# Turning the output columns by a VectorE block transpose instead of a masked matmul, in a decode-step attention and FFN kernel

## The chip, the cores and the metric

The kernel runs on one core of one Trainium2 chip. The metric is the device time of one execution in microseconds (us). The time before is 1287.16 us (median of 6 runs, 1286.88 to 1287.58).

## The reference

One token passes an attention layer with a cache of 32768 positions in 32 heads and, in parallel, a gated FFN. The result is one row of 640 values.

```python
xn = layernorm(x)                                  # x: [1, 1, 640], bf16
q = xn @ wq                                        # 32 heads of 128
p = softmax(q . k_cache * 128 ** -0.5)             # k_cache, v_cache: [1, 32, 32768, 128]
attention = (p . v_cache) @ wo                     # wo: [4096, 640]
ffn = (silu(xn @ w_gate) * (xn @ w_up)) @ w_down   # hidden width 1728
return x + attention + ffn                         # [1, 1, 640], bf16
```

The two caches make up nearly all of the 554 MB that are read.

## The kernel before

SyncE issues the loads into a ring of three large slots. VectorE and TensorE form the scores, ScalarE the exponentials, TensorE the weighted sums. The last weights to be loaded are those of `wo`, in six pieces, and the last sums are accumulated in PSUM (the memory that TensorE writes its sums to) as five columns: `acc[m, c]` holds output `c * 128 + m`. The change concerns only how these columns become the output row.

```python
# TensorE: the last projection, then the turning (fold32[p, m] = 1 where p % 32 == m)
project().then_inc(s_att, 1)                       # acc: [128, NCD], NCD = 5
t.wait_ge(s_fin, 1)
t.matmul(orow_ps, lhsT=outb[:, :, :], rhs=fold32[:, :], start=True, stop=True).then_inc(s_or, 1)

# VectorE: blk[p, a] = 1 where p // 32 == a, RB = 4
v.wait_ge(s_att, 1)
v.tensor_tensor(out=outb[:, :, :], in0=acc[:, :, None].to_broadcast([128, NCD, RB]),
                in1=blk[:, None, :].to_broadcast([128, NCD, RB]), op=ALU.mult).then_inc(s_fin, 1)
v.wait_ge(s_or, 1)
v.tensor_copy(out=orow[:, :], in_=orow_ps).then_inc(s_fin, 1)      # orow: [20, 32] bf16

# SyncE: 20 rows on 20 neighbouring partitions
e.wait_ge(s_fin, 2)
e.dma_start(out[0, 0:1, :].rearrange("o (r m) -> (o r) m", m=32), orow[:, :]).then_inc(s_out, 16)

# GpSimd: the program ends when the store has landed
g.wait_ge(s_out, 16)
# ... everything else is cut here ...
```

The mask spreads each column over four columns, one for each group of 32 partitions. The matmul with `fold32` then adds up each of these 20 columns into a row of 32.

## Time and profile before

| What | Value |
|---|---|
| time, median of 6 runs | 1287.16 us |
| span of the profiled execution | 1285.3 us |
| mean DMA rate | 431 GB/s |
| start of the masking to the issue of the store | 0.68 us |
| issue of the store to the end of the span | 1.4 us |

From the page of the kernel before come its busy times by engine, two of its slice lines (each digit is the busy share of a fortieth of the span, in tenths), and its chain of waits (shares of the span).

```profile
span 1285.3 us, 10032 instructions
PE 1041.2 (81%) x5160; PEld 261.3 (20%) x3240; DVE 672.3 (52%) x409; ACT 52.1 (4%) x139; POOL 2.6 (0%) x18
...
DVE  0855665445665446664446664446654446654441
...
DMA  9999999999999999999999999999999999999998
...
DMA 53%; PE 28%; DVE 12%; issue 6%; DVEq 0%; SPq 0%
```

The DMA engines are busy throughout. A change that touches no transfer of the stream can only gain or lose in the stretch after the last load. The timeline of that stretch follows (start, duration, engine, line, operation, result and operands, count; in brackets the idle time before and what ended it).

```profile
1281.73 1.45 PE L451 MATMUL ps<-ot,ring 128*128 128x1 bf16 x40 [0.72 <-DMA ring<-in_A_wo_dram]
1283.22 0.18 DVE L641 TENSOR_TENSOR outb<-ps,blk 128x20 bf16<-128x20 f32 x1 [11.79 <-PE ps L451]
1283.46 0.09 PEld L476 LDWEIGHTS ps<-fold,outb 128*20 128x20 bf16 x1 [0.36 <-DVE outb L641]
1283.46 0.20 PE L476 MATMUL ps<-fold,outb 128*20 128x32 bf16 x1 [0.27 <-DVE outb L641]
1283.70 0.18 DVE L644 CAST orow<-ps 20x32 bf16<-20x32 f32 x1 [0.29 <-PE ps L476]
1283.90 0.39 SPq L255 DMA_DIRECT2D out_dram<-orow  x1
```

After the last projection come three small instructions on two engines, one after the other, and then the store. The view of the DMA engines over 1283.9 to 1285.1 us, also in 40 slices, shows when the store's packets moved.

```profile
DMA  0000000000000000000000000003010000000000
...
DMA packets 30, 0.00 MB, mean 1 GB/s; under 512 B 30, under 2 KB 30, under 8 KB 30
```

The packets lie in the slices from 27 on, about 0.8 us after the issue began. The trace's records tell more: 20 packets of 64 B and 10 of 4 B, the first 0.805 us after the start of the issue, the last 0.081 us later, and GpSimd's wait ends 0.397 us after that. From the start of the issue to this release it is 1.283 us, nearly twice as long as the turning itself (0.679 us). The chain of waits in the page does not show this part, since it begins at the last instruction that computes.

### The profile page before, as it was taken

The numbers are of one execution on the slowest core, as the hardware profiler recorded it, in microseconds if no ns is written. First come the engines' busy times: TensorE is split into PE (matmuls) and PEld (weight loads), VectorE is DVE, ScalarE is ACT, GpSimd is POOL, SyncE is SP. The second block draws the span as 40 slices with busy tenths as digits, with TensorE's granted clock in tenths as the row PEclk, the third lists the DMA queues.
The fourth block names the chain that finished last, engine by engine and source line by source line (L and its number), as shares of the span: only waits on it lengthen the run. The fifth ranks groups of instructions, "written<-read, shape, count | busy, mean of one in ns | idle before, by whom it ended". The sixth has DMA issues, their size and how long they took to land.

```text
span 1285.3 us, 10032 instructions
## 1 busy us (share of the span) xinstructions
PE 1041.2 (81%) x5160; PEld 261.3 (20%) x3240; DVE 672.3 (52%) x409; ACT 52.1 (4%) x139; POOL 2.6 (0%) x18
## 2 busy tenths in 40 slices
PE   3599777789788789778898877798787798778797
PEld 1022112221112221112221112221112221112227
DVE  0855665445665446664446664446654446654441
ACT  2000000000000000000000000000000000000000
POOL 0000000000000000000000000000000000000000
PEclk9799888898888898888998888898888998888995
DMA  9999999999999999999999999999999999999998
GB/s 424 424 447 429 428 437 435 428 432 439 432 432 432 439 428 432 439 432 432 428 443 428 432 439 432 432 426 445 428 432 439 430 434 426 441 432 432 439 419 364
DMA packets 10987, 554.16 MB, mean 431 GB/s; under 512 B 1247, under 2 KB 1504, under 8 KB 1760
## 3 DMA queue, kind: packets, MB, share of 16 engines
q1 hardware_dynamic: 10974, 554.00, 99.7%
q8 instruction: 9, 0.15, 0.0%
q14 instruction: 2, 0.02, 0.0%
q10 hardware_dynamic: 2, 0.00, 0.0%
HBM read 553.99 MB, written 0.00 MB: 431 GB/s over the span
## 4 chain that ended last, share of the span: by engine, by line
DMA 53%; PE 28%; DVE 12%; issue 6%; DVEq 0%; SPq 0%
DMA ring<-in_A_k_cache_dram 51%; PE ps L358 16%; DVE ring L577 12%; PE ps L310 9%; DMA ring<-in_A_wo_dram 2%; PE ps L342 1%; PE ps L329 1%; PE ps L400 0%; PE ps L394 0%; PE ps L388 0%; PE ps L451 0%; SPq L252 0%; DVEq L577 0%; DVE sc L583 0%; DVE pmax L589 0%
## 5 line engine op out<-in xcount | busy, mean ns | idle before, releaser
L577 DVE TENSOR_TENSOR ring<-ring,qb 128x8192 bf16<-128x8192 bf16 x128 | 557.8, 4421 | 315.8 <-DMA ring<-in_A_k_cache_dram 315.8
L310 PE MATMUL ps<-ring,ident 128*128 128x512 bf16 x1920 | 497.2, 418 | 0.0
L358 PE MATMUL ps<-ring,P 128*4 128x512 bf16 x1920 | 429.0, 379 | 0.0
L329 PE MATMUL ps<-ring,ident 128*128 128x512 bf16 x128 | 55.9, 437 | 220.1 <-DVE ring L577 219.8
L358 PEld LDWEIGHTS ps<-ring,P 128*4 128x4 bf16 x1920 | 158.1, 85 | 230.1
L329 PEld LDWEIGHTS ps<-ring,ident 128*128 128x128 bf16 x128 | 12.6, 98 | 617.6 <-issue 309.7
L583 DVE TENSOR_REDUCE sc<-ps 128x64 f32<-128x512 f32 x128 | 82.3, 686 | 62.8 <-PE ps L310 62.8
L595 DVE TENSOR_SCALAR negb<-ps 128x1 f32<-128x1 f32 x32 | 5.1, 159 | 108.4 <-PE ps L400 108.4
L503 ACT ACTIVATE P<-sc,negb 128x256 bf16<-128x256 f32 x32 | 16.2, 508 | 956.9 <-DVE negb L595 956.9
L592 DVE TENSOR_REDUCE m<-ps 1x1 f32<-1x128 f32 x32 | 8.9, 278 | 85.2 <-PE ps L394 85.2
L380 PEld LDWEIGHTS ps<-identf,o 4*128 4x128 f32 x248 | 30.7, 190 | 13.1 <-issue 13.1
L380 PE MATMUL ps<-identf,o 4*128 4x1 f32 x248 | 33.3, 251 | 0.0
L388 PEld LDWEIGHTS ps<-rsum,ones 128*128 128x128 f32 x64 | 12.1, 190 | 99.3 <-issue 98.5
L494 ACT ACTIVATE o<-ps,rzb 4x512 f32<-4x512 f32 x31 | 21.0, 677 | 6.3 <-PE ps L345 6.3
L301 PE MATMUL ps<-ring 128*128 x40 | 10.6, 432 | 11.2 <-DMA ring<-in_A_wq_dram 11.2
L499 ACT ACTIVATE ocol<-ps 128x1 f32 (+1 forms) x31 | 5.4, 173 | 222.4 <-PE ps L380 222.4
L342 PE MATMUL ps<-ring,P 128*4 x64 | 14.4, 379 | 0.0
L589 DVE TENSOR_REDUCE pmax<-sc 128x1 f32<-128x256 f32 x32 | 13.5, 421 | 0.0
L394 PE MATMUL ps<-identf,pmax 128*1 128x128 f32 x64 | 12.2, 272 | 1.2 <-DVE pmax L589 1.2
L400 PE MATMUL ps<-m,ones 1*128 1x1 f32 x64 | 12.1, 256 | 0.4 <-DVE m L592 0.4
L400 PEld LDWEIGHTS ps<-m,ones 1*128 1x128 f32 x64 | 9.4, 183 | 14.0 <-issue 13.3
L565 DVE RECIPROCAL rzb<-ps 128x1 f32<-128x1 f32 x32 | 5.1, 158 | 8.1 <-PE ps L388 8.1
(75 smaller groups left out, 97.3 us busy)
## 6 DMA issues: line engine op xcount, KB each, us to landing
ring<-in_A_v_cache_dram SPq DMA_DIRECT2D x2, 4096.0 KB, 36.5
ring<-in_A_wq_dram SPq DMA_DIRECT2D x1, 5120.0 KB, 15.5
ring<-in_A_wo_dram SPq DMA_DIRECT2D x3, 1280.0 KB, 24.6
ring<-in_B_w_gate_dram SPq DMA_DIRECT2D x1, 2160.0 KB, 22.6
ring<-in_B_w_up_dram SPq DMA_DIRECT2D x1, 2160.0 KB, 27.9
ring<-in_B_w_down_dram SPq DMA_DIRECT2D x1, 2080.0 KB, 31.0
ring<-in_A_wo_dram SPq DMA_DIRECT2D x1, 800.0 KB, 28.7
ring<-in_A_k_cache_dram SPq DMA_DIRECT2D x32, 41.4
```

Source lines behind the costliest of these rows:

```text
L310: return t.add_instruction(mybir.InstMatmult(start_tensor_calc=False, stop_tensor_calc=stop, tile_size=(128, 128), tile_position=(0, 0), l ...
L329: t.matmul(ob, lhsT=ident[:, :], rhs=src, start=True, stop=False)
L342: t.matmul(O, lhsT=P[:, h % PR, bass.ds(b * (RUN * W) + j, W)], rhs=flat[:, bass.ds(b * (RUN * W * DH) + (s * CE + j * DH), W * DH)], star ...
L358: mm = t.matmul(O, lhsT=P[:, h % PR, j:j + W], rhs=ring[:, s, j * DH:(j + W) * DH], start=(j == 0), stop=(j + W == NJ))
L380: mm = t.matmul(fold_ps, lhsT=o4[:, m * DH:(m + 1) * DH], rhs=identf[0:W, m:m + 1], start=(m == 0), stop=(m == W - 1))
L394: t.matmul(misc[0:1, 0:128], lhsT=pmax[:, h % SR:h % SR + 1], rhs=identf[:, :], start=True, stop=True).then_inc(s_t, 1)
L400: t.matmul(misc[:, 128:129], lhsT=ones[0:1, :], rhs=m1[0:1, h % SR:h % SR + 1], start=True, stop=True).then_inc(s_b, 1)
L494: a.activation(out=o4[:, :], in_=O, func=ACTF.Copy, scale=rzb[0:W, h % SR:h % SR + 1]).then_inc(s_o4, 1)
L503: a.activation(out=P[:, h % PR, :], in_=sc[:, :], func=ACTF.Exp, bias=negb[:, h % SR:h % SR + 1], scale=c_scale, accum_out=rsum[:, h % SR: ...
L577: v.tensor_tensor(out=kh, in0=kh, in1=q[:, None, :].to_broadcast([128, HF, DH]), op=ALU.mult).then_inc(s_mul, 1)
L583: v.tensor_reduce(out=sc[:, i * HF:(i + 1) * HF], in_=bank[i].rearrange("p (j e) -> p j e", e=G), axis=AX.X, op=ALU.add).then_inc(s_red, 1)
L589: v.tensor_reduce(out=pmax[:, h % SR:h % SR + 1], in_=sc[:, :], axis=AX.X, op=ALU.max).then_inc(s_max, 1)
```

## The change

The intent is to spare the masking, the matmul and the changes of engine: VectorE copies the five columns into a zeroed tile, one column at the head of each block of 32, and a block transpose turns each column into rows of 32. Each group of 32 partitions then has its five rows in its first partition, so that the result lies on four partitions, 32 apart.

```diff
-        orow = sbt("orow", [NCD * RB, 32], BF16)
+        orow = sbt("orow", [128, NCD * 32], BF16)
+        ocols = sbt("ocols", [128, NCD * 32], BF16)
-        outb = sbt("outb", [128, NCD, RB], BF16)
...
-                e.dma_start(out[0, 0:1, :].rearrange("o (r m) -> (o r) m", m=32), orow[:, :]).then_inc(s_out, 16)
+                e.dma_start(out[0, 0:1, :].rearrange("o (c g m) -> (o g) c m", c=NCD, m=32),
+                            orow[0:128:32, :].rearrange("g (c m) -> g c m", m=32)).then_inc(s_out, 16)
...
+                done(g.memset(ocols[:, :], 0.0))
...
-                t.wait_ge(s_fin, 1)
-                t.matmul(orow_ps, lhsT=outb[:, :, :], rhs=fold32[:, :], start=True, stop=True).then_inc(s_or, 1)
...
-                v.tensor_tensor(out=outb[:, :, :], in0=acc[:, :, None].to_broadcast([128, NCD, RB]),
-                                in1=blk[:, None, :].to_broadcast([128, NCD, RB]), op=ALU.mult).then_inc(s_fin, 1)
-                v.wait_ge(s_or, 1)
-                v.tensor_copy(out=orow[:, :], in_=orow_ps).then_inc(s_fin, 1)
+                v.tensor_copy(out=ocols[:, :].rearrange("p (c m) -> p c m", m=32)[:, :, 0], in_=acc).then_inc(s_fin, 1)
+                v.wait_ge(s_fin, 1)
+                v.transpose(out=orow[:, :], in_=ocols[:, :]).then_inc(s_fin, 1)
```

Left out are the renumbered counts of the constants' semaphore, and the semaphore `s_or` and the PSUM place `orow_ps`, which are gone.

More of the change, by code (lines that the diff above doesn't have):

```diff
@@ L135, in bass_parallel_sum__gqa_block_cached__swiglu_ffn__decode_kernel @@
         s_twice = sem("twice")
-        s_xr, s_or = sem("xr"), sem("orow")
+        s_xr = sem("xr")
         s_ob, s_op, s_ot = sem("o_blocks"), sem("o_ps"), sem("o_rows")
@@ L216, in bass_parallel_sum__gqa_block_cached__swiglu_ffn__decode_kernel @@
             misc = ps8[:, 7, :]
-            orow_ps = ps8[0:NCD * RB, 5, 128:160]
             ffn = bank[0]
@@ L276, in pool @@
                     done(g.memset(blk[a * 32:(a + 1) * 32, a:a + 1], 1.0))
-                assert n[0] == 6 + 2 * RB
+                done(g.memset(ocols[:, :], 0.0))
+                assert n[0] == 7 + 2 * RB
                 g.wait_ge(s_out, 16)
@@ L620, in dve @@
                                 scalar2=None, op0=ALU.mult).then_inc(s_ov, 1)
-                v.wait_ge(s_const, 6 + 2 * RB)
+                v.wait_ge(s_const, 7 + 2 * RB)
                 v.wait_ge(s_ov, H + 1)
```

## The prediction

> **What bounds the kernel now.** It streams 554 MB. The slices show the 16 DMA engines at 9 tenths nearly everywhere, 431 GB/s on average; TensorE is 81% busy, VectorE 52%. The chain of waits is cache loads (DMA 53%) and the work that frees ring slots. The stream sets the time until about 1281.7 us of the 1285.3 us span, where the last piece of `wo` lands. The change touches only what follows.
>
> **The tail before** (timeline, last 4 us): last projection matmuls 1281.73 to 1283.18; VectorE spreads the columns with a mask, 1283.22, 179 ns; TensorE turns them with one matmul, 1283.46, 202 ns; VectorE copies PSUM to `orow`, 1283.70, 178 ns; SyncE issues the store at 1283.90 (386 ns); its 30 small packets move near 1284.7 to 1284.8, and the span ends at 1285.3. From the start of the masking to the issue of the store: 0.68 us. All of it is on the critical path.
>
> **Removed.** The masked multiply (179 ns), the matmul (202 ns), the PSUM copy (178 ns) and two changes of engine (40 to 60 ns each).
>
> **Added.** A copy of 128x5 from PSUM, strided into `ocols`. Such a copy at the kernel's start took 0.17 us. A VectorE wait on VectorE: dependent FFN gate steps stand 0.04 us apart. The uncertain 128x160 transpose: a 128x128 bf16 VectorE operation took 0.28 to 0.29 us in the tail and a 128x20 one 0.18, about 1 ns per further element, hence an estimate of 0.32 us. The Trainium skill, "VectorE: DVE Perf Modes", section "The three transpose paths", gives 311 ns for 128x128 and says only 32x32 blocks are turned; about 0.34 scaled. No transpose stands in this trace. Sum: 0.17 + 0.04 + 0.33 = 0.54 us plus the hop to SyncE, against 0.68: a gain of about 0.13 us.
>
> **Moved.** The store carries the same 20 runs of 64 B. The Trainium skill, "DMA: Bandwidth & Descriptors", section "Why a DMA increments its semaphore by 16 and not by 1", says that the number of DMA engines is the largest up to 16 dividing both slowest dimensions: 10 before (20 rows), 4 after. The trace agrees for before: 30 packets, 20 of data and 10 of 4 bytes. After I expect 24 packets on 4 engines, five data packets in line on each instead of two. At about 8 ns a packet this costs 0.02 to 0.06 us. Completion (0.5 us from the last packet to the end) stays. The extra GpSimd memset lies near 4.5 us, needed at 1262: free.
>
> **Net**: 0.05 to 0.15 us shorter, 0.01% of the span, below the spread of three runs (0.42). Predicted 1286.9 us, range 1286.2 to 1287.6. Chances: faster by over 2% 0.005, within 2% 0.985, slower 0.01.
>
> **What would show each step right or wrong.** Timeline: no TensorE instruction after the last projection; VectorE copy near 0.17 us, transpose 0.28 to 0.36 us; masking start to store issue 0.50 to 0.58 us instead of 0.68; last matmul to the end of the span about 2.0 us instead of 2.1. DMA view of the last 2 us: 24 packets, not 30. Everything before 1281 us alike.
>
> **What would make it wrong.** A transpose of 0.6 us or more would lose 0.15 us. A store on 4 engines whose issue or completion is longer by some tenths would cancel the gain. The stream's own variation, or a slow execution, can move the whole by more than the change does.

## The result and the profile after

The changed kernel took 1287.57 us (median of 6 runs, 1287.35 to 1287.63), against 1287.16 for the kernel before. The ratio is 1.0003 with a 95% interval of 0.999 to 1.0016. Ratios are the mean time of one kernel's fast runs over that of the other's of the same rounds, so not quite the ratio of the medians quoted. By that interval the two are the same. The execution's end, however, can be read in the trace to about 0.01 us, and there the difference is plain.

The same lines of the page of the changed kernel:

```profile
span 1285.6 us, 10031 instructions
PE 1044.3 (81%) x5159; PEld 261.1 (20%) x3239; DVE 672.4 (52%) x409; ACT 52.1 (4%) x139; POOL 2.8 (0%) x19
...
DVE  0855665445665446664446664446664446654441
...
DMA  9999999999999999999999999999999999999998
...
DMA 53%; PE 30%; DVE 11%; issue 6%; DVEq 0%; SPq 0%
```

The stream is as it was. The timeline of the last stretch of the changed kernel:

```profile
1281.64 1.47 PE L452 MATMUL ps<-ot,ring 128*128 128x1 bf16 x40 [0.74 <-DMA ring<-in_A_wo_dram]
1283.15 0.18 DVE L640 CAST ocols<-ps 128x5 bf16<-128x5 f32 x1 [11.99 <-PE ps L452]
1283.36 0.34 DVE L642 STREAM_TRANSPOSE orow<-ocols 128x160 bf16<-128x160 bf16 x1
1283.73 0.69 SPq L254 DMA_DIRECT2D out_dram<-orow  x1
```

The turning is shorter, as intended: 0.586 us by the records, from the start of the copy to the issue of the store, instead of 0.679. But the issue itself takes 0.69 us instead of 0.39. The DMA view of the changed kernel, over 1284.53 to 1285.33 us:

```profile
DMA  0000000000000000000000000121000000000000
...
DMA packets 24, 0.00 MB, mean 2 GB/s; under 512 B 24, under 2 KB 24, under 8 KB 24
```

There are 24 packets instead of 30, and they begin to move near 1285.0 us, 1.28 us after the issue began. The records give the parts of the store:

| Part of the store, us | Before | Changed |
|---|---|---|
| issue on SyncE | 0.386 | 0.688 |
| end of the issue to the first packet | 0.419 | 0.593 |
| first packet to the last | 0.081 | 0.093 |
| last packet to GpSimd's release | 0.397 | 0.360 |
| whole, start of the issue to the release | 1.283 | 1.734 |

The turning gained 0.09 us, and the store lost 0.45, so that the tail from the first VectorE instruction to the release went from 1.962 to 2.320 us. This 0.36 us is of the size of the 0.41 us between the medians, but that is no proof of it: the six runs before spread over 0.70 us.

### The profile page after: what moved, and what is told of

It is laid out like the page before. It is cut to its first block, busy times and chain, and to the rows that moved or that the text cites. A ratio compares the mean times of both kernels' runs of the same rounds, so it can differ in the third digit from the quotient of the medians.

```text
span 1285.6 us, 10031 instructions
## 1 busy us (share of the span) xinstructions
PE 1044.3 (81%) x5159; PEld 261.1 (20%) x3239; DVE 672.4 (52%) x409; ACT 52.1 (4%) x139; POOL 2.8 (0%) x19
## 4 chain that ended last, share of the span: by engine, by line
DMA 53%; PE 30%; DVE 11%; issue 6%; DVEq 0%; SPq 0%
DMA ring<-in_A_k_cache_dram 51%; PE ps L359 16%; PE ps L311 11%; DVE ring L576 11%; DMA ring<-in_A_wo_dram 2%; PE ps L343 1%; PE ps L330 1%; PE ps L401 0%; PE ps L395 0%; PE ps L389 0%; PE ps L452 0%; SPq L251 0%; DVEq L576 0%; DVE sc L582 0%; DVE pmax L588 0%
```

## The experiments

What made the store's issue longer? The store was changed in four ways at once: it has three dimensions instead of two, it is shared by 4 DMA engines instead of 10, its source rows stand 32 partitions apart, and they were written by the transpose. Eleven kernels and a repetition of the changed one tell these apart. They ran four at a time on one chip, in the order of the groups below (of the last four, e10_packed_4stores is told last). The edits are shown shortened: allocations, constants and counts of semaphores are left out. In each group the kernel before ran on the same chip 9 times: medians 1286.86 (first group), 1287.03 (second) and 1287.26 us (third).

All the kernels with one last store are gathered here, by the trace's records. "Engines" is the number of 4 B packets, which goes with the number of engines used. The last column begins at the end of the last VectorE instruction, so that it holds nothing of the turning.

| Kernel | Source rows, partitions | Dims | Engines | Issue us | VectorE end to release us |
|---|---|---|---|---|---|
| before | 20, neighbours | 2 | 10 | 0.386 | 1.311 |
| changed | 4, step 32 | 3 | 4 | 0.688 | 1.761 |
| changed, again | 4, step 32 | 3 | 4 | 0.696 | 1.773 |
| e1_flat_rows | 4, step 32 | 2 | 4 | 0.654 | 1.714 |
| e3_10x2x32 | 10, neighbours | 3 | 10 | 0.377 | 1.305 |
| e4_19rows | 19, neighbours | 2 | 1 | 0.327 | 1.356 |
| e5_matmul_4x5x32 | 4, neighbours | 3 | 4 | 0.342 | 1.258 |
| e7_rehearsed | 4, step 32 | 3 | 4 | 0.552 | 1.750 |
| e9_before_rehearsed | 20, neighbours | 2 | 10 | 0.317 | 1.373 |
| e6_step2 | 4, step 2 | 3 | 4 | 0.812 | 1.884 |
| e8_20rows_step4 | 20, step 4 | 2 | 10 | 0.906 | 2.000 |
| e11_matmul_step32 | 4, step 32 | 3 | 4 | 0.696 | 1.772 |
| e12_across | 4, neighbours | 3 | 4 | 0.343 | 1.243 |

### Dimensions: e1_flat_rows

```diff
-out[0, 0:1, :].rearrange("o (c g m) -> (o g) c m", c=NCD, m=32), orow[0:128:32, :].rearrange("g (c m) -> g c m", m=32)
+out[0, 0:1, :].rearrange("o (g n) -> (o g) n", g=4), orow[0:128:32, :]
```

> The changed kernel with its store written as 4 rows of 160 contiguous elements (320 B), two dimensions instead of three; the output comes out in a wrong order on purpose. Before, the issue of the store took 386 ns on SyncE and 1.28 us passed from its start to GpSimd's release at the end; changed, 688 ns and 1.73 us. Theory D (the third dimension of the access pattern makes the issue long): the issue falls to 0.35 to 0.42 us, start of issue to the end to about 1.3 us, and the kernel ends about 0.45 us earlier than the changed one, some 0.1 us ahead of before. Theory E (four DMA engines instead of ten make it long): it stays near 0.65 to 0.7 us and 1.7 us. Theory P (the source rows stand 32 partitions apart, or the transpose's output lands late): it also stays near 0.69 us.

The output was in the wrong order, as intended. The time was 1287.28 us (5 runs, ratio to before 1.0004, interval 0.999 to 1.0017), and the issue stayed long, in the timeline of this run:

```profile
1282.95 0.35 DVE L642 STREAM_TRANSPOSE orow<-ocols 128x160 bf16<-128x160 bf16 x1
1283.33 0.65 SPq L254 DMA_DIRECT2D out_dram<-orow  x1
```

With two dimensions, and with only 4 data packets of 320 B instead of 20 of 64 B, the issue is 0.03 us shorter. The third dimension is not the cause, and neither is the number of small runs.

### Neighbouring rows in three dimensions: e3_10x2x32

```diff
-orow[0:128:32, :].rearrange("g (c m) -> g c m", m=32)
+orow[0:10, 0:64].rearrange("g (t m) -> g t m", m=32)      # out: "o (t g m) -> (o g) t m", t=2
```

> The changed kernel, but its store reads partitions 0 to 9, two runs of 64 B each: three dimensions, ten DMA engines, 20 runs of 64 B, neighbouring partitions; wrong output on purpose. Theory D (dimensions): the issue takes 0.6 to 0.7 us and the path from issue to the end about 1.7 us, as in the changed kernel, though ten engines share it (30 packets). Theory E (number of engines): 0.35 to 0.42 us and about 1.3 us, as before. Theory P (partitions 32 apart): also as before.

The output was wrong, as intended; one run, 1287.04 us. The timeline of this run:

```profile
1283.26 0.35 DVE L642 STREAM_TRANSPOSE orow<-ocols 128x160 bf16<-128x160 bf16 x1
1283.63 0.38 SPq L254 DMA_DIRECT2D out_dram<-orow  x1
```

This store reads the same transposed tile in three dimensions and its issue is as short as before. So the tile that the transpose wrote is not slow to store. What is left is the number of engines or the step.

### One engine: e4_19rows

```diff
-out[0, 0:1, :].rearrange("o (r m) -> (o r) m", m=32), orow[:, :]
+out[0, 0:1, 0:608].rearrange("o (r m) -> (o r) m", m=32), orow[0:19, :]
```

> The kernel before, storing only 19 of its 20 rows (the last 32 outputs are not written, on purpose): 19 is prime, so the whole store should go to one DMA engine, in two dimensions: 20 packets instead of 30. Theory D (dimensions): the issue stays at 0.35 to 0.42 us, and the end moves by under 0.2 us. Theory E (rows in line on one engine): the issue or the path to the first packet grows by at least what four engines did, 0.3 to 0.5 us or more.

The last 32 outputs were not written, as intended; one run, 1287.18 us. There were 20 packets, one of them of 4 B, so by that count one engine did it all. The issue was shorter than before, 0.327 us, and the packets took 0.132 us instead of 0.081. Fewer engines did not lengthen the issue. Nineteen rows in line on one engine instead of two cost 0.05 us, less than the prediction's 8 ns a packet would give (17 more of them: 0.14 us).

### The changed kernel's store without the transpose: e5_matmul_4x5x32

```diff
-t.matmul(orow_ps, lhsT=outb[:, :, :], rhs=fold32[:, :], ...)         # outb: acc * blk, [128, 20]
+t.matmul(orow_ps, lhsT=blk[:, :], rhs=outb[:, :, :], ...)            # outb: acc * fold32, [128, 160]; orow: [4, 160]
...
+e.dma_start(out "o (c g m) -> (o g) c m", orow[:, :].rearrange("g (c m) -> g c m", m=32))
```

> The kernel before with a masked matmul, but arranged to give 4 rows of 160 on partitions 0 to 3, stored by the same 4x5x32 pattern as in the changed kernel; correct output; no transpose. Theory D and theory E: the issue takes about 0.69 us and issue start to the end about 1.73 us, so the tail is about 0.45 to 0.6 us longer than before (the masking is over 160 elements instead of 20 per partition, some 0.15 us more). Theory P (partitions 32 apart, or the transpose itself): the issue is back at 0.39 us and issue start to the end at 1.28 us.

The output was correct and the time 1287.25 us (5 runs; ratio 1.0003, interval 0.9989 to 1.0017). The timeline of this run:

```profile
1282.82 0.32 DVE L642 TENSOR_TENSOR outb<-ps,fold 128x160 bf16<-128x160 f32 x1 [11.20 <-PE ps L452]
...
1283.20 0.29 PE L477 MATMUL ps<-outb,blk 128*4 128x160 bf16 x1 [0.42 <-DVE outb L642]
1283.53 0.31 DVE L645 CAST orow<-ps 4x160 bf16<-4x160 f32 x1 [0.39 <-PE ps L477]
1283.87 0.34 SPq L255 DMA_DIRECT2D out_dram<-orow  x1
```

The store has the same shape and 4 engines, but its rows lie on partitions 0 to 3, and it is issued in 0.34 us. Its path to the release, 1.258 us, is even a little shorter than before. The turning is longer here, because each instruction works on 160 elements per partition.

### A rehearsal: e7_rehearsed and e9_before_rehearsed

Such a store could also be slow only because it is the first of its kind. SyncE idles for 24 us before the real store, and a first store fits there.

```diff
+                e.dma_start(out "o (c g m) -> (o g) c m", blank[0:128:32, :] "g (c m) -> g c m").then_inc(s_reh, 16)
+                e.wait_ge(s_reh, 16)
                 e.wait_ge(s_fin, 2)
```

In e9_before_rehearsed the first store has the shape of the kernel before and takes its rows from `ident`.

> The changed kernel, with one more store of the same pattern (4 rows, 32 partitions apart, 4x5x32) issued by SyncE while it idles for 24 us before the end; its zeros are overwritten by the real store; correct output. So far the issue took 0.65 to 0.69 us when the source rows stood 32 partitions apart, and 0.33 to 0.39 us when they were neighbours, whatever the dimensions and the number of DMA engines. Theory F (the first use of such a pattern is slow): the last store's issue falls to 0.35 to 0.4 us and issue start to GpSimd's release to about 1.25 us; the kernel gains 0.45 us on the changed one and ends about 0.1 us before the kernel before. Theory S (a partition step costs in every use): the last issue stays at 0.65 to 0.69 us and both stores show it; no gain.

> The kernel before with a rehearsal of its own store (20 neighbouring rows of 32) in the same idle time of SyncE; correct output. Theory F in a wide form (the first store of any kind is slow): the last issue falls from 0.386 us to about 0.3 and the end comes earlier by 0.1 us or more. Theory S, and theory F for stepped patterns alone: issue 0.37 to 0.39 us and issue start to release 1.28 us as before; time within 0.1 us of before.

Both were correct. The changed kernel with rehearsal took 1287.39 us (ratio to before 1.0002, interval 0.9988 to 1.0016), the kernel before with rehearsal 1286.94 us (0.9999, interval 0.9986 to 1.0013). The two waits ahead of the last store now stand as an instruction of their own some 0.08 us before the issue, so the shorter issues in the table (0.552 and 0.317 us) are not a gain: from the end of VectorE to the release it is 1.750 us, against 1.761 to 1.773 without the rehearsal, and 1.373 against 1.311 for the kernel before. So most of the cost returns in the second use: with the rehearsal in both kernels the changed one's path is 0.377 us longer, without it 0.450 us. Whether the 0.07 us between these belong to a first use, one trace of each does not settle. The rehearsal's own issue (3.58 us, and 4.40 in e9_before_rehearsed) came right after those of six loads, so it tells nothing of the step, and the expectation that both stores would show it was not tested.

### Other steps: e6_step2 and e8_20rows_step4

```diff
-orow[0:128:32, :]         # both wrong on purpose
+orow[0:8:2, :]            # e6_step2, 4x5x32
+orow[0:80:4, 0:32]        # e8_20rows_step4, stored as before: 20x32
```

> The changed kernel with the store's source rows 2 partitions apart instead of 32 (partitions 0, 2, 4, 6; wrong output on purpose). Any step other than 1 costs: issue 0.65 to 0.69 us, issue start to release about 1.7 us. Only rows in different groups of 32 partitions cost: 0.33 to 0.36 us and about 1.23 us.

> The changed kernel storing 20 rows of 32 elements that stand 4 partitions apart (0 to 76; wrong output on purpose), two dimensions, ten DMA engines, as before except for the step. A fixed cost of a step: issue 0.386 + 0.3 = about 0.69 us. A cost of each row (0.3 us over 4 rows, 75 ns a row): issue about 1.9 us. No cost of a step of 4: 0.386 us.

One run each: 1287.39 and 1287.68 us. The timeline of e8_20rows_step4:

```profile
1283.30 0.34 DVE L641 STREAM_TRANSPOSE orow<-ocols 128x160 bf16<-128x160 bf16 x1
1283.67 0.91 SPq L254 DMA_DIRECT2D out_dram<-orow  x1
```

A step inside one group of 32 costs too, and in this one run more than one of 32: the issue took 0.812 us at a step of 2. Twenty rows at a step of 4 took 0.906 us, 0.52 more than twenty neighbours. The cost is thus not 75 ns for each row whatever the step (20 rows would have come to 1.9 us), and it is not a fixed 0.3 us either. How it depends on the step stays open.

### The step alone: e11_matmul_step32, with the changed kernel again

```diff
-orow_ps, lhsT=blk[:, :]         # e5: rows on partitions 0 to 3
+orow_ps, lhsT=spread4[:, :]     # [128, 128]: rows on partitions 0, 32, 64, 96
-orow[:, :].rearrange("g (c m) -> g c m", m=32)
+orow[0:128:32, :].rearrange("g (c m) -> g c m", m=32)
```

> The masked matmul of the earlier run with 4 rows of 160 on partitions 0 to 3, but the rows put on partitions 0, 32, 64 and 96 by a wider weight; no transpose, correct output, the store's pattern that of the changed kernel exactly. If the partition step alone is the cause: the issue goes from 0.342 to about 0.69 us and issue start to release from 1.23 to about 1.73 us. If the transpose is needed for it: 0.34 and 1.23 us.

> The changed kernel once more, on the chip of these runs: issue 0.65 to 0.70 us, issue start to release 1.70 to 1.75 us, time 0.3 to 0.5 us over the kernel before.

Both were correct. The matmul kernel with the step took 1287.83 us (5 runs; ratio to before 1.0005, interval 0.9992 to 1.0019), the changed kernel 1287.38 us (5 runs; 1.0002, interval 0.9988 to 1.0016). The timeline of e11_matmul_step32:

```profile
1283.70 0.33 DVE L649 CAST orow<-ps 128x160 bf16<-128x160 f32 x1 [0.41 <-PE ps L481]
1284.05 0.70 SPq L256 DMA_DIRECT2D out_dram<-orow  x1
```

With no transpose in the kernel, the step takes the issue from 0.342 to 0.696 us and the path from VectorE's end to the release from 1.258 to 1.772 us. These are the changed kernel's values to within 0.02 us. This shows the cause: the partition step of the store's source. The two matmul kernels ran on different chips, but each of these chips showed both kinds of issue: 0.654 us (e1_flat_rows) beside 0.342, and 0.343 (e12_across) beside 0.696.

Of the whole times, this repetition shows how far they carry. The changed kernel was 0.12 us over the median of before, not the 0.3 to 0.5 that I had expected, although its tail was as long as the first time. The 9 runs of the kernel before spread from 1286.88 to 1287.53 us in this group, which is wider than the effect.

### No step, with the transpose: e12_across

```diff
-orow[0:128:32, :]
+orow[30:34, :]            # wrong on purpose
```

> The changed kernel storing 4x5x32 from partitions 30 to 33: neighbours, but across a border of 32 (wrong output on purpose). The step is the cause: issue 0.33 to 0.36 us, issue start to release 1.23 us. Crossing a group of 32 is the cause (for the 32-step): issue about 0.69 us.

One run, 1286.83 us. The timeline of e12_across:

```profile
1282.99 0.18 DVE L640 CAST ocols<-ps 128x5 bf16<-128x5 f32 x1 [11.12 <-PE ps L452]
1283.20 0.34 DVE L642 STREAM_TRANSPOSE orow<-ocols 128x160 bf16<-128x160 bf16 x1
1283.57 0.34 SPq L254 DMA_DIRECT2D out_dram<-orow  x1
```

Crossing a border of 32 cost nothing here: the issue took 0.343 us. This kernel differs from the changed one in the rows of the store alone. With the transpose as it is and neighbouring rows, copy to issue took 0.586 us and issue to release 1.215, in all 1.80 us, against 1.962 in the kernel before. So the change would have gained 0.16 us if the transpose left its rows side by side. It does not, and this output is wrong; it is a bound, not a version.

### A way around the step: e10_packed_4stores

```diff
-v.tensor_copy(out=ocols[:, :].rearrange("p (c m) -> p c m", m=32)[:, :, 0], in_=acc)
+v.tensor_copy(out=ocols[:, 0:NCD], in_=acc)              # ocols, orow: [128, 32]
-e.dma_start(...)                                         # one store
+for g in (0, 2): e.dma_start(out "o (c g m) -> (o g) c m"[g], orow[32 * g:32 * g + NCD, :])   # SyncE
+for g in (1, 3): a.dma_start(out "o (c g m) -> (o g) c m"[g], orow[32 * g:32 * g + NCD, :])   # ScalarE
```

> The transpose kept, the partition step avoided: the 5 columns lie side by side in one block, so the transpose covers 128x32 instead of 128x160 and leaves 5 neighbouring rows in each group of 32 partitions; four stores of 5x32, two issued by SyncE and two by ScalarE; correct output. If the step is the cause: every issue takes 0.30 to 0.40 us (no step), the transpose about 0.2 us instead of 0.345, copy to first issue 0.46 us instead of 0.59, and the second issue of each queue starts 0.35 to 0.55 us after the first; first issue to the end about 1.6 to 1.8 us; in all 0.05 to 0.25 us shorter than the changed kernel, and 0.1 to 0.3 us longer than before. If the transposed rows themselves were slow to store: issues of 0.65 us, and the kernel ends later than the changed one.

The output was correct and the time 1288.04 us (5 runs; ratio 1.0007, interval 0.9993 to 1.002), the slowest of all. The timeline of e10_packed_4stores:

```profile
1282.95 0.17 DVE L645 CAST ocols<-ps 128x5 bf16<-128x5 f32 x1 [11.40 <-PE ps L453]
1283.15 0.21 DVE L647 STREAM_TRANSPOSE orow<-ocols 128x32 bf16<-128x32 bf16 x1
1283.39 1.06 SPq L255 DMA_DIRECT2D out_dram<-orow  x2
1283.39 0.63 ACTq L530 DMA_DIRECT2D out_dram<-orow  x2
```

The first part went about as expected: the single issues took 0.28 to 0.36 us, and the transpose 0.21. The expected end failed. SyncE's second issue began 0.767 us after its first (ScalarE's 0.314), the last packets moved 1.96 us after the first issue began, and GpSimd was released only at 2.77 us, instead of the 1.6 to 1.8 us expected. The wait from the last packet to the release doubled, to 0.80 us; why is not settled. Four small stores cost more than the step did.

No experiment points to a version that is correct and faster than both kernels.

## Why the prediction was right or wrong

- **What bounds the kernel: right.** The DMA slices are the same before and after and the chain nearly so, and the change moved the whole time by 0.03%. It was within 2% as predicted. That the range of 1286.2 to 1287.6 us held, by 0.03 us, is luck: a small gain was predicted and a small loss came, and the range was wide enough for both.
- **Removed and added: right, but for a few hundredths.** The copy was predicted at 0.17 us and took 0.179, the transpose at 0.33 and took 0.345, masking start to store issue at 0.50 to 0.58 and took 0.586, just above. The gain of this part was 0.09 us instead of the predicted 0.13: of the missing 0.04 us, some 0.02 are the two instructions and some 0.02 the change to SyncE (0.027 us), for which the sum left 0.01. The Trainium skill, "VectorE: DVE Perf Modes", section "The three transpose paths", gives 311 ns for 128x128; the prediction's "0.34 scaled" is an estimate from it, with 1 ns for each of the 32 further elements. A line through the measured 345 ns (128x160) and 213 ns (128x32) gives 312 for it.
- **Number of DMA engines: right, its price smaller.** The Trainium skill, "DMA: Bandwidth & Descriptors", section "Why a DMA increments its semaphore by 16 and not by 1", gives the rule, that the number is the largest up to 16 which divides both slowest dimensions. The 4 B packets were 10, 4 and 1 for 20, 4 and 19 rows, as it says. Five packets in line instead of two lengthened the movement by 0.012 us, under the predicted 0.02 to 0.06.
- **"Moved": wrong, and with it the sign of the net.** The step that failed is the cost of the store: that it "carries the same 20 runs of 64 B" is so (20 packets of 64 B before and after), but not that it therefore costs only "0.02 to 0.06 us" more. The runs showed 0.45 us in its place. Of this, 0.30 us lie in the issue and 0.17 between its end and the first packet; the completion after the last packet, which "stays" in the prediction, did so (0.397 and 0.360 us). The prediction compared runs and engines, and overlooked that the rows no longer lie on neighbouring partitions.
- **Net: wrong in direction.** Instead of 0.05 to 0.15 us shorter, the tail became 0.36 us longer. The "last matmul to the end of the span about 2.0 us instead of 2.1" became about 2.5. The prediction had named a store "whose issue or completion is longer by some tenths" among what would make it wrong, but not its cause.

What is shown is that the step is the cause: adding it to the matmul kernel gives the whole loss, and taking it away under the transpose takes it away. Why a step costs time in the issue is not shown by these runs.

## What to carry to other kernels

When a change rearranges data on the chip, look at how the next store must read it: here a cheaper turning left its rows 32 partitions apart, and the partition step in the store cost 0.45 us, five times what the turning had saved. At the end of this kernel the issue and completion of the last store are on the critical path (1.28 us, against 0.68 us for the turning), and the chain of compute instructions does not show them. And differences of some tenths of a microsecond in a long kernel are found in the trace of the stretch concerned, not in the whole times, which here spread by as much or more.

## What the Trainium skill lacked or had wrong

- "DMA: Bandwidth & Descriptors": its rules for kernel authors warn of a later dimension that steps whole partitions, but no page says that a step of more than one partition in the first dimension slows a store. In the table of stores above, such stores were issued in 0.55 to 0.91 us, and neighbouring rows in 0.32 to 0.39 us; from the end of the issue to the first packet 0.59 to 0.64 us passed instead of 0.42 to 0.46.
- The same page, section "Anatomy of one DMA — SWDGE (gpsimd) path", puts most of a DMA's fixed 2.0 us into the receipt after the last byte. That is measured on another issuing path; for SyncE's the page has a first-byte latency, but no such split. For this 1280 B store, issued by SyncE, 0.40 of 1.28 us came after the last packet and 0.81 before the first.
- "VectorE: DVE Perf Modes" gives the transpose's duration at one size only. Two more are 213 ns for 128x32 and 345 ns for 128x160.
